# Weight loads of a fused attention and feed-forward kernel: from GpSimd DMAs that cast to SyncE DMAs with a cast on VectorE and ScalarE

## The chip, the cores and the metric

The kernel runs on one core of one Trainium2 chip. A core has five engines with queues of their own: TensorE (PE, matmuls; PEld is its weight load), VectorE (DVE), ScalarE (ACT), GpSimd (POOL) and SyncE (SP), and 16 DMA engines. Each engine takes its instructions in order and waits on semaphores. The metric is the time of one execution on the device in microseconds; the median of seven runs is given. Less is better.

## The reference

Block-wise decaying linear attention over 4 batches of 8 heads, 768 positions and 64 features, followed by a feed-forward layer with a Silu, 512 to 2048 to 512, over all 3072 tokens. Inputs and output are float32. `Dmask`, `lam_pow` and `rev_pow` hold powers of the head's decay `lam`: by distance within the block (zero ahead of the diagonal), by position from its start, and by position from its end; `lam_block` is the decay of a whole block.

```python
for b in range(nb):                       # blocks of 64 positions
    qb, kb, vb = (q[:, :, sl], k[:, :, sl], v[:, :, sl])
    intra = np.einsum('bhic,bhjc->bhij', qb, kb) * Dmask[None]
    intra = np.einsum('bhij,bhjd->bhid', intra, vb)
    inter = np.einsum('bhid,bhde->bhie', qb * lam_pow[None], kv_state)
    out[:, :, sl] = intra + inter
    kb_dec = kb * rev_pow[None]
    kv_state = lam_block[None, :, None, None] * kv_state + np.einsum('bhsd,bhse->bhde', kb_dec, vb)
...
x = out, heads side by side, one row a token
h = x @ w_in
g = h * (1.0 / (1.0 + np.exp(-h)))
return g @ w_out
```

## The kernel before

The 3072 tokens are 24 chunks of 128 (six to a batch) and ten groups of 256 or 384. For each chunk the kernel scales q and k by powers of the decay, transposes them, forms masked scores, adds the state's part and writes the attention output, in bf16 and transposed, into the group's tile `xt`. For each group it multiplies `xt` with `w_in_bf` (the up projection: L488 for groups of 256, L511 for groups of 384), applies Silu on ACT (L493, L515) into tiles `g`, and multiplies those with `w_out_bf` (the down projection, L537) into `o_ps`, which DVE copies to `ob` (L541) and SP stores.

The schedule is written out by hand. The opening, chunks 0 to 3 and the up projections of groups 0 and 1, is the string `ORDER`, in which each word is one operation: `qc:2,1,P` scales half 1 of the q pair of chunks 2 and 3 on POOL (L304), `kc` and `vc` do the same or a plain cast for k and v (L214, L152, L148; a last letter `s` means scaled, `u` unscaled), `tq` and `tk` transpose on PE (L369, L237), `qt` and `kt` copy the transposes out of PSUM, `s` forms scores (L251), `m` masks them on DVE (L257), `d` adds to the state (L289), `kv` copies it, `o` forms the output (L265, L270), `x` copies it to `xt`. `u:g,b,h` is 8 matmuls of 256 columns of the up projection for group g, block b of four output tiles, half h of the contraction; `g:` closes a bank with a Silu; `z:n` is n warm-up matmuls on zeros (L592). `w:i` loads piece i of w_in: 512 columns and half of the contraction, the piece that `u:g,b,h` with 2b + h = i needs. The letters D, A, P name the engine; the words give every engine's order, since each engine takes its own in the order of the string.

Weights are loaded by POOL with DMAs that cast from float32 to bf16 on the way, so they land where the matmuls read them (L144): eight w_in pieces of 512 KB in DRAM, four w_out pieces of 1 MB. q, k and v of chunks 0 to 5 come as pairs of blocks (`load_pair`, L187; 512 KB) or singly (`load_1`, L196; 256 KB) on SP, six pairs at the start. Two one-element DMAs from `xt` and `g` into a tile `gate` on SP (L620, L624) hold back the loads queued behind them until those tiles are written. The pair tiles are a ring of five and one tile with the tag `gate`.

After `ORDER` come the down projections of groups 0 and 1 (`down0(kk, ...)`: contraction tiles 4kk to 4kk+3) with the attention of chunks 4 and 5 between them: q and k scaled on POOL (L304, L309), `pe_tq`, `pe_tk` (L383), key copies into the zero-padded `ktbd` on DVE, scores `st_s` (L435), output `st_o` (L466). The padded tiles `ktbd` and `vpad` are zeroed first, two of each on DVE (L629, L630) and two on POOL (`clear_halves`, L164, L165); `clear_halves(0, 1)` comes again later for another layout. From chunk 6 on, `stretch` interleaves up projections, attention pieces and down projections by position; nothing of the change lies there.

```python
    for i in range(2):
        nc.vector.memset(ktbd[i], 0.0)
        nc.vector.memset(vpad[i], 0.0)
    clear_halves(2, 3)
...
    down0(0, 2, 3, 0, 1)
    prep_q1(4, 1), prep_q1(4, 0), prep_k(4), prep_k(5)
    down0(1, 2, 3, 0, 1)
    tq4 = pe_tq(4, "att")
```

Of the kernel before, what the change touches and what calls it, by code (L numbers as in the profile page):

```python
# [7 lines left out]
F32 = mybir.dt.float32  # L8
BF16 = mybir.dt.bfloat16
# [4 lines left out]

GROUPS = [256, 256, 256, 256, 256, 384, 384, 384, 384, 256]
# [4 lines left out]

ORDER = """
wl qc:0,0,P qc:0,1,D z:14 tq:0,att vc:0,0,P,s kc:0,0,D,u qt:0,0,D kc:0,1,A,u tk:0,1,h qt:0,1,A kt:0,1,D tk:0,0,att
qc:2,1,P kt:0,0,A z:2 s:0,1,att,o qc:2,0,P s:0,0,o,h vc:0,1,D,s d:0 m:0,1,0,D m:0,0,0,D m:0,1,1,D kv:0,A d:1 kc:2,1,D,u
kc:2,0,A,u m:0,0,1,D tq:2,att qt:2,1,D tk:2,0,o w:0 w:1 kv:1,A kt:2,0,D tk:2,1,h qt:2,0,A kt:2,1,A o:0,att,h vc:2,1,D,s
s:2,1,att,o m:2,1,1,D s:2,0,o,att m:2,0,1,D m:2,1,0,D vc:2,0,P,s x:0,A d:2 x:1,A u:0,0,0,h,h m:2,0,0,D w:2 kv:2,A d:3
kv:3,A u:0,0,1 g:0,0,1 o:2,att,att x:2,A w:3 w:4 x:3,D g:0,0,0 u:0,1,0,o,o u:0,1,1 g:0,1,0 g:0,1,1 u:1,0,0,h,h w:5
u:1,0,1 g:1,0,0 u:0,2,0,o,o u:0,2,1 w:6 g:1,0,1 g:0,2,1 w:7 u:1,3,0,h,h u:1,3,1 g:0,2,0 g:1,3,0 u:1,2,0,o,o u:1,2,1
g:1,3,1 g:1,2,0 g:1,2,1 u:0,3,0,h,h u:0,3,1 g:0,3,1 u:1,1,0,o,o u:1,1,1 g:1,1,1 g:1,1,0 g:0,3,0
# [4 lines left out]
def kernel(  # L33
# [10 lines left out]
    nc = tc.nc  # L44
# [29 lines left out]

    iota_i = const.tile([128, 2 * NB], mybir.dt.int32)
# [27 lines left out]
    NKV = 4  # L103
# [32 lines left out]

    def load_w(which, *pieces):
        for i in pieces:
            if which == "in":
                b, h = divmod(i, 2)  # L140
                dst, src = [t[:, 2 * h:2 * h + 2, 512 * b:512 * b + 512] for t in (w_in_bf, w_in_r)]
            else:
                dst, src = [t[:, 4 * i:4 * i + 4, :] for t in (w_out_bf, w_out_r)]
            nc.gpsimd.dma_start(out=dst, in_=src)  # L144
# [9 lines left out]
    mask2 = const.tile([128, BLK], F32)  # L154

# [24 lines left out]
    def load_q(c):  # L180

        load_pair(q, c, rawq, "gate")

    def load_pair(src, c, dst, tag="pair"):
        b, blk = divmod(c, NB)
        t = io.tile([128, H, 2, D], F32, name="pair", tag=tag, bufs={"pair": 5, "gate": 1}[tag])
        nc.sync.dma_start(out=t.rearrange("p h r d -> p h (r d)"),  # L187
                          in_=src[b, :, blk * BLK:(blk + 2) * BLK, :].rearrange("h (p r) d -> p h (r d)", r=2))
        dst[c] = t
# [9 lines left out]
    def load_k(c):  # L199
        rawk[c] = load_1(k, c, "kf", 6)  # L200

    def load_v(c):
        vraw[c] = load_1(v, c, "vf", 6)

    def load_c(c):
        rawq[c] = load_1(q, c, "qf", 4)
        load_k(c)
        load_v(c)
# [357 lines left out]
    for c in (0, 2):  # L566
        load_pair(q, c, rawq), load_pair(k, c, rawk), load_pair(v, c, vraw, "gate" if c else "pair")
# [20 lines left out]
    def op_z(n, tag="kv"):  # L588
# [8 lines left out]
        "w": lambda i: load_w("in", i), "u": op_u, "g": op_g, "z": op_z,  # L597
# [21 lines left out]
    gate = const.tile([128, 1], BF16)  # L619
    nc.sync.dma_start(out=gate[0:1, :], in_=xt[1][0:1, 0, 0:1])  # L620
    load_q(4)
    load_k(4), load_k(5)
    load_w("out", 0, 1, 2, 3)
    nc.sync.dma_start(out=gate[0:1, :], in_=gt[1, 0][0:1, 0:1])  # L624
    load_v(4), load_v(5)
    load_c(6)
    load_c(7)
    for i in range(2):
        nc.vector.memset(ktbd[i], 0.0)  # L629
        nc.vector.memset(vpad[i], 0.0)  # L630
    clear_halves(2, 3)
    for j in range(2):
        nc.gpsimd.tensor_copy(mask2[64 * j:64 * j + 64, :], mask[0:64, :])
# [15 lines left out]
    st_s(4)  # L649
    down0(2, 0, 1)  # L650
# [93 lines left out]
```

## Time and profile before

| | us |
|---|---|
| median of 7 runs | 219.43 |
| lowest, highest | 219.04, 222.48 |
| the profiled execution's own time | 222.45 |
| its span | 220.7 |
| PE busy in the span | 209.0 (95%) |
| DVE, ACT, POOL busy | 98.9, 95.7, 66.3 |
| first up-projection matmul starts | 17.64 |
| first down-projection matmul starts | 35.82 |

The span is from the first to the last recorded instruction; the rest of the execution's time lies around it. A line of the timeline gives the start in us, the duration in us, engine, source line, operation, output and inputs with their sizes, how many it stands for, and in brackets the idle time of the engine before it with what ended it. A window line gives a stretch, its length, the busy us of each engine with its number of instructions, the granted clock of TensorE, the mean busy share of the DMA engines (it can pass 1 where transfers overlap) and GB/s written. A DMA that casts counts with the bytes that it writes.

### The profile page before, as it was taken

The page shows a single profiled execution, that of the slowest core. Times are in us where ns is not written, and L with a number is a line of the kernel's source. Part 1 is how long each engine was busy: PE and PEld are TensorE (multiplying, and loading weights), DVE is VectorE, ACT ScalarE, POOL GpSimd, SP SyncE. Part 2 cuts the span into 40 slices and gives each one's busy share as a digit, 9 for nine tenths or more (in the row PEclk, how much of TensorE's full clock was granted, in tenths as well). Part 3 has the DMA queues.
Part 4 walks back from the last instruction along what each step waited for, and adds up shares of the span by engine and source line. Part 5 has one row for each costly group of instructions (what it writes and reads, how often), then busy time and mean ns, then how long its engine had stood idle before and what let it go on. Part 6 is the DMA issues. An engine that isn't in the chain of part 4 may idle for free.

```text
span 220.7 us, 4469 instructions
## 1 busy us (share of the span) xinstructions
PE 209.0 (95%) x1792; PEld 134.9 (61%) x1792; DVE 98.9 (45%) x239; ACT 95.7 (43%) x179; POOL 66.3 (30%) x83
## 2 busy tenths in 40 slices
PE   7878998999969999999999999999999999999994
PEld 2465775456846787776666566556655555566654
DVE  2693400067697467476665363624761333001121
ACT  4773554043542455554555454445444443432210
POOL 5599623144943333323403333202000000000000
PEclk9976999999997999999999999999999999999999
DMA  4979999987999999999988699928610110011112
GB/s 116 328 170 153 178 215 203 202 202 177 252 255 183 237 170 203 222 201 218 220 142 218 166 191 224 217 73 184 128 48 0 52 48 37 13 48 48 48 50 97
DMA packets 93209, 33.86 MB, mean 153 GB/s; under 512 B 78596, under 2 KB 90244, under 8 KB 93188
## 3 DMA queue, kind: packets, MB, share of 16 engines
q1 hardware_dynamic: 88756, 29.37, 57.6%
q0 software_dynamic: 4288, 4.20, 12.2%
q8 instruction: 14, 0.23, 0.5%
q14 instruction: 7, 0.06, 0.1%
q10 hardware_dynamic: 144, 0.00, 0.0%
HBM read 27.27 MB, written 6.29 MB: 152 GB/s over the span
## 4 chain that ended last, share of the span: by engine, by line
PE 76%; DMA 14%; DVE 4%; SPq 2%; POOL 1%; ACT 0%; issue 0%; DVEq 0%
PE o_ps L537 32%; PE h_ps L511 19%; PE h_ps L488 13%; DMA kf<-in_k_dram 9%; PE op L466 5%; PE sp L435 3%; DMA pair<-in_q_dram 3%; DMA w_in_bf<-in_moe_w_in_dram 2%; SPq L187 2%; DVE vpad L346 2%; PE kv_ps L411 2%; PE o_part L554 2%; POOL qb L304 1%; DVE ktbd L152 1%; POOL kb L309 0%
## 5 line engine op out<-in xcount | busy, mean ns | idle before, releaser
L537 PE MATMUL o_ps<-w_out_bf,g 128*128 128x512 bf16 x368 | 92.1, 380 | 0.8 <-ACT g L493 0.8
L537 PEld LDWEIGHTS <-g 128*128 128x128 bf16 x368 | 35.1, 98 | 32.0 <-issue 1.4
L515 ACT ACTIVATE g<-h_ps 128x384 bf16<-128x384 f32 x64 | 31.4, 490 | 46.7 <-PE h_ps L511 46.2
L488 PE MATMUL h_ps<-xt,w_in_bf 128*128 128x256 bf16 x384 | 49.7, 280 | 1.8 <-DMA w_in_bf<-in_moe_w_in_dram 1.8
L511 PE MATMUL h_ps<-xt,w_in_bf 128*128 128x384 bf16 x256 | 50.6, 326 | 0.0
L493 ACT ACTIVATE g<-h_ps 128x512 bf16<-128x512 f32 x48 | 27.9, 596 | 37.8 <-PE h_ps L488 37.7
L488 PEld LDWEIGHTS <-w_in_bf 128*128 128x128 bf16 x384 | 37.0, 100 | 10.1 <-DMA w_in_bf<-in_moe_w_in_dram 2.6
L315 POOL TENSOR_TENSOR qb<-qf,lam_fwd 128x512 bf16<-128x512 f32 x18 | 18.8, 1042 | 65.4 <-DMA qf<-in_q_dram 62.8
L541 DVE COPY ob<-o_ps 128x512 f32<-128x512 f32 x23 | 15.9, 691 | 47.7 <-PE o_ps L537 47.6
L511 PEld LDWEIGHTS <-w_in_bf 128*128 128x128 bf16 x256 | 23.7, 98 | 17.2
L442 DVE TENSOR_TENSOR ss<-sp,mask 128x512 bf16<-128x512 f32 (+1 forms) x40 | 21.0, 567 | 22.1 <-PE sp L435 22.0
L309 POOL TENSOR_TENSOR kb<-kf,lam_bwd 128x512 bf16<-128x512 f32 x20 | 20.9, 1045 | 7.9 <-DMA kf<-in_k_dram 7.8
L346 DVE COPY vpad<-vb 64x256 bf16<-64x256 bf16 x72 | 19.7, 273 | 1.6
L152 DVE CAST kvbd<-kv_ps 64x256 bf16<-64x256 f32 x32 | 13.5, 421 | 12.6 <-PE kv_ps L411 12.3
L474 ACT ACTIVATE xt<-op 128x512 bf16<-128x512 f32 x20 | 11.9, 597 | 13.7 <-PE op L466 13.0
L435 PEld LDWEIGHTS <-ktbd 128*128 128x128 bf16 x160 | 9.6, 100 | 5.0 <-DVE ktbd L152 1.9
L435 PE MATMUL sp<-qt,ktbd 128*128 128x128 bf16 (+1 forms) x160 | 10.6, 211 | 1.3 <-DVE ktbd L152 1.3
L466 PE MATMUL op<-ss,vpad 128*128 128x128 bf16 (+1 forms) x160 | 10.5, 208 | 1.2 <-DVE vpad L346 1.2
L148 ACT ACTIVATE vb<-vf 128x512 bf16<-128x512 f32 x18 | 11.2, 622 | 0.0
L152 DVE COPY ktbd<-tk 64x512 bf16<-64x512 bf16 x4 | 1.7, 422 | 20.6 <-PE tk L383 20.6
L466 PEld LDWEIGHTS <-vpad 128*128 128x128 bf16 x160 | 8.8, 98 | 1.9 <-DVE vpad L346 1.7
L152 DVE COPY ktbd<-kn 64x512 bf16<-64x512 bf16 x32 | 9.7, 302 | 0.4
(77 smaller groups left out, 124.2 us busy)
## 6 DMA issues: line engine op xcount, KB each, us to landing
out_dram<-ob SPq DMA_DIRECT2D x23, 256.0 KB, 3.2
kf<-in_k_dram SPq DMA_DIRECT2D x20, 256.0 KB, 4.0
vf<-in_v_dram SPq DMA_DIRECT2D x20, 256.0 KB, 4.4
qf<-in_q_dram SPq DMA_DIRECT2D x18, 256.0 KB, 3.4
w_in_bf<-in_moe_w_in_dram POOLq DMA_DIRECT2D x8, 256.0 KB, 8.3
w_out_bf<-in_moe_w_out_dram POOLq DMA_DIRECT2D x4, 512.0 KB, 18.5
pair<-in_q_dram SPq DMA_DIRECT2D x3, 512.0 KB, 6.1
pair<-in_k_dram SPq DMA_DIRECT2D x2, 512.0 KB, 6.3
```

Source lines behind the costliest of these rows:

```text
L152: nc.vector.tensor_copy(dst, src)
L309: VG[e].tensor_tensor(kb, rawk.pop(c).rearrange("s (p j) d -> s p j d", j=2), decay(lam_bwd, c % NB), op=AL.mult)
L315: nc.gpsimd.tensor_tensor(qb, rawq.pop(c).rearrange("s (p j) d -> s p j d", j=2), decay(lam_fwd, c % NB), op=AL.mult)
L346: nc.vector.tensor_copy(vh[64 * j:64 * j + 64, :, h, j, :], vb[64 * h:64 * h + 64, :, j, :])
L435: nc.tensor.matmul(sp[:, p, :], lhsT=lhsT, rhs=qt[:, p, a:], start=True, stop=True)
L442: VG[e].tensor_tensor(ss, sp, m[:, None, :n].to_broadcast([128, 4, n]), op=AL.mult)
L466: nc.tensor.matmul(dst, lhsT=lhsT, rhs=rhs, start=(i == 0), stop=(i >= len(terms) - NP), skip_group_check=True)
L488: nc.tensor.matmul(hps[g, i][:, a:a + 256], lhsT=w_in_bf[:, ko, m * 128:(m + 1) * 128], rhs=xt[g][:, ko, :], start=(ko == 0 and u == 0), s ...
L493: nc.scalar.activation(gg.rearrange("p u n -> p (u n)"), hps[g, i], AF.Silu)
L511: nc.tensor.matmul(hp[:, a:z], lhsT=w_in_bf[:, ko, m * 128:(m + 1) * 128], rhs=xt[g][:, ko, a:z], start=(ko == 0 and a == 0), stop=(ko == ...
L515: nc.scalar.activation(gg, hp[:, :n], AF.Silu)
L537: nc.tensor.matmul(o, lhsT=gt[g, ko][:, mt * BLK:(mt + 1) * BLK], rhs=w_out_bf[:, ko, :], start=(ko == 0), stop=(ko == KO_OUT - 1))
```

## The change

Weights come as float32 on SP's queue into the tiles of the pair ring and are cast to bf16 by DVE or ACT: `load_w` now only loads, `cast_w` casts. `LOADS` gives the order on SP: w_in pieces stand between and behind the q, k, v pairs, then six w_out pieces of 512 KB, then the loads of chunk 4 and so on. The ring has six tiles for all of these. In `ORDER` the word `w` is now a cast of half a piece with its engine, and the order of the opening is another one: key scaling comes first and chunk 0 scales k instead of v, there is one more pair of warm-up matmuls, and the up projections run in another sequence. The two gate DMAs are gone with their tile; a tile `pad` of 32 bytes a partition stands among the constants. The zero fills that POOL did before the down projection are done by DVE, and the copies of `mask` to `mask2` on POOL move to the front.

```diff
-wl qc:0,0,P qc:0,1,D z:14 tq:0,att vc:0,0,P,s kc:0,0,D,u qt:0,0,D kc:0,1,A,u tk:0,1,h qt:0,1,A kt:0,1,D tk:0,0,att
-qc:2,1,P kt:0,0,A z:2 s:0,1,att,o qc:2,0,P s:0,0,o,h vc:0,1,D,s d:0 m:0,1,0,D m:0,0,0,D m:0,1,1,D kv:0,A d:1 kc:2,1,D,u
-kc:2,0,A,u m:0,0,1,D tq:2,att qt:2,1,D tk:2,0,o w:0 w:1 kv:1,A kt:2,0,D tk:2,1,h qt:2,0,A kt:2,1,A o:0,att,h vc:2,1,D,s
-s:2,1,att,o m:2,1,1,D s:2,0,o,att m:2,0,1,D m:2,1,0,D vc:2,0,P,s x:0,A d:2 x:1,A u:0,0,0,h,h m:2,0,0,D w:2 kv:2,A d:3
-kv:3,A u:0,0,1 g:0,0,1 o:2,att,att x:2,A w:3 w:4 x:3,D g:0,0,0 u:0,1,0,o,o u:0,1,1 g:0,1,0 g:0,1,1 u:1,0,0,h,h w:5
-u:1,0,1 g:1,0,0 u:0,2,0,o,o u:0,2,1 w:6 g:1,0,1 g:0,2,1 w:7 u:1,3,0,h,h u:1,3,1 g:0,2,0 g:1,3,0 u:1,2,0,o,o u:1,2,1
-g:1,3,1 g:1,2,0 g:1,2,1 u:0,3,0,h,h u:0,3,1 g:0,3,1 u:1,1,0,o,o u:1,1,1 g:1,1,1 g:1,1,0 g:0,3,0
+wl kc:0,1,D,s z:14 tk:0,1,att qc:0,1,P vc:0,0,A,u qc:0,0,D z:2 tq:0,o kt:0,1,D qt:0,0,A qt:0,1,D kc:0,0,P,s tk:0,0,o z:2
+s:0,1,att,h qc:2,1,P m:0,1,0,D m:0,1,1,D vc:0,1,A,u kt:0,0,A d:0 kv:0,A s:0,0,o,o m:0,0,0,D kc:2,1,A,u d:1 m:0,0,1,D
+qc:2,0,P tq:2,h vc:2,0,P,s w:0,1,D kc:2,0,A,u tk:2,1,att kt:2,1,D qt:2,0,A o:0,h,att w:0,0,D qt:2,1,A vc:2,1,P,s tk:2,0,o
+x:0,A s:2,1,att,o x:1,D m:2,1,0,D kt:2,0,A u:0,0,0,h,h s:2,0,att,att w:1,1,A w:1,0,D m:2,1,1,D u:0,0,1 w:2,0,D kv:1,A d:2
+w:2,1,A u:0,1,0,o,o m:2,0,1,D m:2,0,0,D kv:2,A w:3,1,D d:3 kv:3,D g:0,0,1 w:3,0,A o:2,att,att w:4,0,D u:0,1,1 g:0,0,0
+w:4,1,A x:3,D x:2,A u:0,2,0,h,h w:5,0,D w:5,1,D g:0,1,1 u:0,2,1 g:0,1,0 w:7,0,D g:0,2,0 w:6,1,D g:0,2,1 u:1,1,0,o,o
+u:1,1,1 g:1,1,0 g:1,1,1 u:1,0,0,h,h w:6,0,D u:1,0,1 g:1,0,0 w:7,1,D g:1,0,1 u:0,3,0,o,o u:0,3,1 g:0,3,0 u:1,3,0,h,h
+u:1,3,1 g:0,3,1 g:1,3,1 g:1,3,0 u:1,2,0,o,o u:1,2,1 g:1,2,1 g:1,2,0
...
+LOADS = "Q0 K0 V0 Q2 K2 W0 V2 W1 W2 W3 W4 W5 W6 W7"
...
+    pad = const.tile([128, PAD], mybir.dt.uint8, name="pad")
...
+    wtmp = {}
+
+    def w_piece(which, i, a, b):
+        if which == "in":
+            c, h = divmod(i, 2)
+            return slice(2 * h + a, 2 * h + b), slice(512 * c, 512 * c + 512)
+        return slice(2 * i + a, 2 * i + b), slice(0, DM)
+
     def load_w(which, *pieces):
         for i in pieces:
-            if which == "in":
-                b, h = divmod(i, 2)
-                dst, src = [t[:, 2 * h:2 * h + 2, 512 * b:512 * b + 512] for t in (w_in_bf, w_in_r)]
-            else:
-                dst, src = [t[:, 4 * i:4 * i + 4, :] for t in (w_out_bf, w_out_r)]
-            nc.gpsimd.dma_start(out=dst, in_=src)
+            ko, f = w_piece(which, i, 0, 2)
+            t = io.tile([128, 2, 512], F32, name="pair", tag="pair", bufs=6)
+            nc.sync.dma_start(out=t, in_=(w_in_r if which == "in" else w_out_r)[:, ko, f])
+            wtmp[which, i] = t
+
+    def cast_w(which, i, e="D", part=None):
+        a, b = (0, 2) if part is None else (part, part + 1)
+        ko, f = w_piece(which, i, a, b)
+        move(e, (w_in_bf if which == "in" else w_out_bf)[:, ko, f], wtmp[which, i][:, a:b, :])
...
     mask2 = const.tile([128, BLK], F32)
+    for j in range(2):
+        nc.gpsimd.tensor_copy(mask2[64 * j:64 * j + 64, :], mask[0:64, :])
...
-        load_pair(q, c, rawq, "gate")
-
-    def load_pair(src, c, dst, tag="pair"):
+        load_pair(q, c, rawq)
+
+    def load_pair(src, c, dst):
         b, blk = divmod(c, NB)
-        t = io.tile([128, H, 2, D], F32, name="pair", tag=tag, bufs={"pair": 5, "gate": 1}[tag])
+        t = io.tile([128, H, 2, D], F32, name="pair", tag="pair", bufs=6)
...
-    for c in (0, 2):
-        load_pair(q, c, rawq), load_pair(k, c, rawk), load_pair(v, c, vraw, "gate" if c else "pair")
+    for word in LOADS.split():
+        if word[0] == "W":
+            load_w("in", int(word[1]))
+        else:
+            load_pair(*{"Q": (q, int(word[1]), rawq), "K": (k, int(word[1]), rawk), "V": (v, int(word[1]), vraw)}[word[0]])
+    load_w("out", *range(6))
+    load_q(4)
+    load_k(4), load_k(5)
+    load_w("out", 6, 7)
+    load_v(4), load_v(5)
+    load_c(6)
+    load_c(7)
...
-        "w": lambda i: load_w("in", i), "u": op_u, "g": op_g, "z": op_z,
+        "w": lambda i, h, e: cast_w("in", i, e, h), "u": op_u, "g": op_g, "z": op_z,
...
-    gate = const.tile([128, 1], BF16)
-    nc.sync.dma_start(out=gate[0:1, :], in_=xt[1][0:1, 0, 0:1])
-    load_q(4)
-    load_k(4), load_k(5)
-    load_w("out", 0, 1, 2, 3)
-    nc.sync.dma_start(out=gate[0:1, :], in_=gt[1, 0][0:1, 0:1])
-    load_v(4), load_v(5)
-    load_c(6)
-    load_c(7)
-    for i in range(2):
+    for i in range(6):
+        cast_w("out", i)
+    for i in range(NKV):
         nc.vector.memset(ktbd[i], 0.0)
         nc.vector.memset(vpad[i], 0.0)
-    clear_halves(2, 3)
-    for j in range(2):
-        nc.gpsimd.tensor_copy(mask2[64 * j:64 * j + 64, :], mask[0:64, :])
...
     st_s(4)
+    cast_w("out", 6), cast_w("out", 7, "A")
     down0(2, 0, 1)
```

## The prediction

> **What bounds the kernel now.** I read the page's parts 1 and 2 first, then the chain of waits, then the windows and the timeline of the first 70 us. Columns of part 2 are 40 slices of 5.5 us.
>
> ```profile
> span 220.7 us, 4469 instructions
> PE   7878998999969999999999999999999999999994
> DMA  4979999987999999999988699928610110011112
> PE 76%; DMA 14%; DVE 4%; SPq 2%; POOL 1%; ACT 0%; issue 0%; DVEq 0%
> ```
>
> From about 70 us TensorE is never idle by more than an issue gap, and the waits after 75 us name no wait of PE at all. So the end moves only by what PE loses or gains before 70 us: a microsecond won there is one won at the end. The change touches only that part. The windows of 2 us (columns: stretch, its length, busy us and instructions of PE, weight loads, DVE, ACT, POOL, then granted clock, DMA share, GB/s written) show the opening:
>
> ```profile
> 8.00:10.00 2.00, 1.87 (x34) 1.28 (x34) 1.57 (x4) 1.41 (x3) 0.77 (x1) 1.00 1.08 317
> ...
> 12.00:14.00 2.00, 1.59 (x36) 1.44 (x35) 2.00 (x6) 1.39 (x3) 2.00 (x3) 1.00 0.64 191
> 14.00:16.00 2.00, 1.97 (x67) 1.65 (x66) 2.00 (x4) 1.89 (x4) 1.98 (x3) 0.50 0.71 83
> 16.00:18.00 2.00, 1.03 (x30) 0.82 (x22) 2.00 (x4) 1.03 (x3) 2.00 (x4) 0.50 0.85 124
> ```
>
> The DMA engines, full until 12 us, fall to 0.64 to 0.85 until 18 us: the six q, k, v pairs have landed and the first weights, issued by POOL at 12.74 behind its own tensor work, have not. The first up-projection matmul waits for them, and later ones again, as the timeline says:
>
> ```profile
> 12.74 1.61 POOL L144 DMA_DIRECT2D w_in_bf<-in_moe_w_in_dram  x2
> ...
> 17.64 1.89 PE L488 MATMUL h_ps<-xt,w_in_bf 128*128 128x256 bf16 x8 [0.97 <-DMA w_in_bf<-in_moe_w_in_dram]
> ...
> 29.69 6.29 PE L488 MATMUL h_ps<-xt,w_in_bf 128*128 128x256 bf16 x56 [0.44 <-DMA w_in_bf<-in_moe_w_in_dram]
> ...
> 37.64 6.20 PE L537 MATMUL o_ps<-w_out_bf,g 128*128 128x512 bf16 x28 [0.80 <-ACT g L493]
> ...
> 46.44 0.40 PE L383 MATMUL tk<-ident,kb 128*128 128x128 bf16 x4 [0.20 <-POOL kb L309]
> ```
>
> The 128 matmuls of the opening's up projection ("u" items) run from 17.64 to 35.8, 18.2 us, though at the undisturbed pace of 0.87 us per 8 they are 14.0. DVE shows 0.00 busy from 30 to 44 us.
>
> **What the skill says.** "DMA: Bandwidth & Descriptors", section "Issuing engines are not separate DMA queues": all queues run on the same 16 engines, so a move from POOL to SP adds no bandwidth. The trace agrees: the share is 1.19 to 1.23 in nearly every window from 24 to 42 us with both queues in use. "SBUF — State Buffer", section "SBUF: two separate sides": VectorE in a two-port mode, or with two SBUF inputs, and GpSimd exclude each other for a whole instruction. The trace agrees: L214 on DVE took 1.55 and 1.72 us beside a POOL operation where the same form at L304 took 0.69. "TensorE: Matmul & The Clock Gate", Part 1: the array falls to half clock after an idle window of about 3.4 us. The trace shows 0.50 between 14 and 20 us, where 8 matmuls took 1.89 instead of 0.87.
>
> **The change part by part.** Sizes: 512 KB is one unit (a q, k or v pair, a w_in piece, a new w_out piece).
>
> 1. Loads on SP. Readers in the trace are released by K0 at 7.55, V0 at 9.23, Q2 at 10.75, K2 at 12.49, V2 by 14.3: 1.6 us a unit, the n-th landing near 4.4 + 1.6n. After the change nothing interrupts this stream: W0 is n=6 (14.0), V2 15.6, W1 17.2, then one each 1.6 us to W7 at 26.8, the first six w_out pieces 28.4 to 36.4, Q4 38.0, K4 and K5 39 and 40, the last w_out pieces 43.2. It can be quicker: from 24 to 44 us the trace wrote about 205 GB/s, near 4.1 MB; less Q4, K4 and K5 (1.05 MB) these are some 3.05 MB of cast weights, read as twice that, so about 7.15 MB read in 20 us, 355 GB/s and 1.5 us a unit. I work with 1.6 and keep 1.5 as the good end. The 8 + 4 POOL issues of 0.74 us vanish from POOL's queue; two stood before the k, v work of chunk 2. Both gate copies on SP go too.
>
> 2. Staging ring. Five pair tiles and one gate tile, filled seven times before, become six tiles filled 23 times; SP waits in order until the piece in a slot has been cast. By the readers' times: W2 waits for Q2's two POOL multiplies (10.75 + 2.08 = 12.9), W4 for V2's (15.6 + 2.08 = 17.7), W6 for W0's casts (about 16). Each is before the stream has used up the three units already queued (4.8 us), so I count nothing. A slot may be held 6 x 1.6 = 9.6 us.
>
> 3. Start of attention. On DVE the multiply of K0 now stands before that of Q0, so Q0's half waits until 7.55 instead of running at 6.27; with a POOL multiply of 1.04 in its way it ends near 10.0 (before: 7.0). Transposes 10.4, ACT and DVE copies 11.0, scores 11.2 (before 9.68): 1.5 us late. Four masks of 0.68 on DVE from 11.6 end at 14.3, output matmuls near 15.0, the x copies, behind two casts on DVE, at 16.6. W0 is cast by 15.9. So the first u begins at 16.6, against 17.64: 1.0 us gained. The added pair of warm matmuls (about 0.6) fills a PE wait.
>
> 4. Casts. 12 of w_in on DVE x 0.56 (row of the 128x512 cast, 0.535 to 0.591) = 6.8 us; 4 on ACT x 0.62 = 2.5; 7 of w_out on DVE, 128x1024, bounded by 0.59 and twice 0.56: I take 1.1, sum 7.9; one on ACT, 1.1. Not one is free by nature: they lie on the way from landing to matmul. But each costs PE only its lag where PE waits for that piece. Until about 25 us it does: u of piece W1 near 17.95, W2 19.4, o of chunk 2 20.8, W3 21.6, W4 22.6, W5 24.8. From there PE works through the u items of group 1, ending near 34.4 (ten items of 0.87 and 0.9 of waits for W6 and W7 after 24.8), or 33.8 with units of 1.5 us. Against 35.8 that is 1.4 to 2.0 gained.
>
> 5. Down projection. Before, its fifth matmul waits from 36.7 to 37.64 for the last Silu to free a bank; the new order closes those g items an earlier block ahead, so this 0.9 goes. Then 40 matmuls of 0.216 and 16 transposes (0.9) lead to the last key transpose: 34.4 + 9.5 = 43.9 against 46.44 + 0.2. W_out casts are ready in time (piece 5: 36.4 + 1.1 = 37.5, needed at 41.8).
>
> 6. Zero fills. Four POOL fills of 0.97 go from a time when POOL waits 7.9 us for Q4 afterwards: worth nothing. Four DVE fills of 0.49 are added, behind the casts: 8 fills end at 37.5 + 3.9 = 41.4. The copies of chunk 4's keys stand behind them, wanted at 42.9. Hidden with 1.5 us to spare. Q4 and both K cost POOL 2.08 + 2.08 after 38.0: 42.2, wanted at 43.7, also hidden.
>
> 7. The 256-byte boundaries. The removed gate tile occupied one 32-byte slot ahead of the weights; the added pad is 32 bytes. In the two built programs the weight, pair, k, v, q and output tiles have equal addresses, all multiples of 256 already. Only masks and padded k, v tiles move. This part does nothing to DMA: 0.
>
> Sum: 1.4 (u end) + 0.9 (bank wait) + 0.4 (the key transpose stood at 46.44, though the four matmuls begun at 45.22 end, at 0.216 each, at 46.1) = 2.7 at the slow unit; 3.3 at the fast one. I take 3.0. Later loads (chunks 6, 7) come earlier by as much, since the same stream brings them. PE's stalls between 57 and 66 us (waits on ktbd and vpad, 2.6 us) I leave as they are.
>
> The profiled execution has span 220.7 and own time 222.45, 1.75 around it; it would become 219.45. The median of the seven runs is 219.43; the profiled one also shows clock 0.66 between 65 and 70 us. I set the same difference against the median: 216.4.
>
> **Rivals.**
> (a) Ring and in-order casts starve the stream; slower. A slot is held from issue to landing (some 4.4 us without backlog, from the 4.0 and 4.4 of k and v issues) plus cast wait plus cast 1.1. To lose, K5 must be multiplied at 46.4 instead of 42.2, less the 1.5 spare that costs nothing at first: 4.2 us over 15 units, so 1.9 us each, a hold of 11.3 us, a cast wait of nearly 6 us. At a unit of 2.1 us K5 comes 7.5 late and the end 3.3 later than before: 222.7. For: cast of W6 stands behind the first half of W7 on DVE, and casts stand among attention steps. Against: step 4's waits are below 2 us.
> (b) The gain is mostly eaten: attention starts later still, because DVE and POOL collide on K0, and PE at half clock runs the W1 to W4 items at 1.75 us each. Then u ends near 35.5, 0.3 is won there and 0.9 at the bank wait: 218.2.
> (c) Two stalls more go: with chunks 6 and 7 landed early, POOL's multiplies no longer collide with DVE's vpad copies (L346, four in 3.92 us near 59): 2 us more, 214.4.
> (d) Everything cancels within 0.2%: 219.4.
>
> **How the numbers follow.** Forecast 0.55, (a) 0.17, (b) 0.13, (c) 0.10, (d) 0.05. The likeliest case's own range is 215.1 to 217.7. Leaving out the upper part of (a) and the lower of (c), the range is 214.4 to 219.9. What can be told from no change is 0.2%, 0.44 us. Faster 0.55 + 0.13 + 0.10 = 0.78, same 0.05, slower 0.17.
>
> **What would show it.** Right: DMA share stays at 1 from 4 to 45 us; first u near 16.6; down projection from 33 to 34.5 with no wait after its fourth matmul; last key transpose near 43. Wrong: SP waiting on casts for microseconds, a drop of the DMA share between 14 and 40 us, PE waiting on ktbd behind the fills, or a first u after 18.

## The result and the profile after

| | before | after |
|---|---|---|
| median, us | 220.1 (217.89 to 223.05, 60 runs) | 217.74 (216.63 to 219.96, 23 runs) |
| ratio | | 0.9907, 95% interval 0.9891 to 0.9923 |
| the profiled execution's own time, us | 222.45 | 217.2 |
| its span, us | 220.7 | 215.5 |

The ratio and its interval leave out executions more than 1.5% above the fastest of their kernel, so the ratio is not quite the quotient of the medians. The change makes the kernel 0.93% faster, about 2.05 us. The two profiled executions are 5.2 us apart, two and a half times as much. So one of the two is not a usual one, and before any line of them is compared this has to be settled: the first experiment does it.

The page of the changed kernel (its first line, the DMA row of the 40 slices, which are 5.4 us each here, and the engines' shares of the chain that ended last):

```profile
span 215.5 us, 4511 instructions
...
DMA  4999999998997779998999999839311011011112
...
PE 84%; DVE 6%; DMA 6%; ACT 2%; issue 1%; SPq 0%; DVEq 0%
```

The 7 in the third slice of the DMA row of before (11 to 16.5 us) is a 9 now, and the DMA's share of the chain falls from 14% to 6%: the end is seldom traced back to a load now. The windows of the opening (stretch, its length, busy us and instructions of PE, weight loads, DVE, ACT, POOL, then granted clock, DMA share, GB/s written) say the same:

```profile
12.00:14.00 2.00, 1.47 (x51) 1.24 (x51) 1.19 (x2) 1.29 (x5) 0.70 (x1) 0.70 1.04 338
14.00:16.00 2.00, 2.00 (x66) 1.77 (x66) 2.00 (x6) 1.97 (x4) 0.51 (x1) 1.00 1.13 383
16.00:18.00 2.00, 1.21 (x25) 0.90 (x26) 2.00 (x4) 1.99 (x6) 1.72 (x2) 1.00 1.01 384
```

The share is 1.01 to 1.13 where it was 0.64 to 0.85, and the clock is full from 14 us on, where in the first profile it was a half until 20. Only from 18 to 20 us does the share drop, to 0.77. The timeline of the changed kernel, DVE and PE lines in order of time:

```profile
7.62 0.69 DVE L233 TENSOR_TENSOR kp<-pair,lam_bwd 128x512 bf16<-128x512 f32 x1 [2.70 <-DMA pair<-in_k_dram]
8.22 1.53 DVE L323 TENSOR_TENSOR qb<-pair,lam_fwd 128x512 bf16<-128x512 f32 x1
12.81 2.48 DVE L276 TENSOR_TENSOR ss<-sp,mask_p 128x512 bf16<-128x512 f32 x4 [0.88 <-PE sp L270]
15.88 0.94 DVE L169 CAST w_in_bf<-pair 128x512 bf16<-128x512 f32 x1
16.74 0.68 DVE L169 CAST xt<-op 128x512 bf16<-128x512 f32 x1
17.47 1.05 PE L507 MATMUL h_ps<-xt,w_in_bf 128*128 128x256 bf16 x8 [0.79 <-DVE xt L169]
22.62 12.02 PE L507 MATMUL h_ps<-xt,w_in_bf 128*128 128x256 bf16 x104
34.48 7.07 PE L556 MATMUL o_ps<-w_out_bf,g 128*128 128x512 bf16 x32
43.78 0.39 PE L402 MATMUL tk<-ident,kb 128*128 128x128 bf16 x4
```

Of the four PE waits that the prediction showed, the last three are gone. The first up-projection item starts hardly earlier than before (17.47 against 17.64) and now waits for the copy of the attention output to `xt`, not for weights. The remaining 104 matmuls from 22.62 on are one line. That hides waits too short for a line of their own: near 24.6 and 25.0 us two matmuls start 0.37 and 0.34 us behind the one before, where 0.11 is usual, because the casts of W5 are late. The waits of the weight loads show them (waiting engine and line, whom it waited for, us in total, times, longest):

```profile
PEld L507 <- DVE w_in_bf L169: 0.6, 2, 0.4
```

So about 0.5 us is still lost to weights there, and none behind it. The down projection's first 32 matmuls are one line too, so the wait for a Silu's bank is gone. The last key transpose of the opening, that of chunk 5, stands at 43.78.

### The profile page after: what moved, and what is told of

It is laid out like the page before. It is cut to its first block, busy times and chain, and to the rows that moved or that the text cites. A ratio compares the mean times of both kernels' runs of the same rounds, so it can differ in the third digit from the quotient of the medians.

```text
span 215.5 us, 4511 instructions
## 1 busy us (share of the span) xinstructions
PE 206.3 (96%) x1794; PEld 133.3 (62%) x1794; DVE 115.2 (53%) x261; ACT 98.6 (46%) x184; POOL 55.2 (26%) x68
## 4 chain that ended last, share of the span: by engine, by line
PE 84%; DVE 6%; DMA 6%; ACT 2%; issue 1%; SPq 0%; DVEq 0%
PE o_ps L556 36%; PE h_ps L530 19%; PE h_ps L507 15%; PE op L485 5%; PE sp L454 3%; DMA pair<-in_k_dram 3%; DMA pair<-in_moe_w_in_dram 3%; PE o_part L573 2%; PE kv_ps L430 2%; DVE ktbd L169 1%; DVE ss L461 1%; PE tq L388 1%; DVE qb L323 1%; DVE vpad L365 1%; ACT kvbd L165 1%
## 5 line engine op out<-in xcount | busy, mean ns | idle before, releaser
L556 PEld LDWEIGHTS <-g 128*128 128x128 bf16 x368 | 35.0, 98 | 31.2 <-issue 0.4
L507 PE MATMUL h_ps<-xt,w_in_bf 128*128 128x256 bf16 x384 | 47.9, 273 | 0.9 <-DVE xt L169 0.8
L507 PEld LDWEIGHTS <-w_in_bf 128*128 128x128 bf16 x384 | 36.1, 98 | 8.4 <-DVE xt L169 0.9
L530 PEld LDWEIGHTS <-w_in_bf 128*128 128x128 bf16 x256 | 23.7, 98 | 17.2
L461 DVE TENSOR_TENSOR ss<-sp,mask 128x512 bf16<-128x512 f32 (+1 forms) x40 | 21.0, 566 | 16.6 <-PE sp L454 16.3
L365 DVE COPY vpad<-vb 64x256 bf16<-64x256 bf16 x72 | 20.4, 283 | 1.6
L169 DVE CAST kvbd<-kv_ps 64x256 bf16<-64x256 f32 x34 | 14.3, 421 | 11.9 <-PE kv_ps L430 10.7
L169 DVE COPY ktbd<-kn 64x512 bf16<-64x512 bf16 x32 | 15.6, 486 | 0.4
L323 POOL TENSOR_TENSOR qb<-pair,lam_fwd 128x512 bf16<-128x512 f32 x5 | 5.1, 1041 | 21.9 <-DMA pair<-in_q_dram 20.3
```

The lines of the kernel that those rows point to most:

```text
L169: nc.vector.tensor_copy(dst, src)
L365: nc.vector.tensor_copy(vh[64 * j:64 * j + 64, :, h, j, :], vb[64 * h:64 * h + 64, :, j, :])
L461: VG[e].tensor_tensor(ss, sp, m[:, None, :n].to_broadcast([128, 4, n]), op=AL.mult)
L507: nc.tensor.matmul(hps[g, i][:, a:a + 256], lhsT=w_in_bf[:, ko, m * 128:(m + 1) * 128], rhs=xt[g][:, ko, :], start=(ko == 0 and u == 0), s ...
L530: nc.tensor.matmul(hp[:, a:z], lhsT=w_in_bf[:, ko, m * 128:(m + 1) * 128], rhs=xt[g][:, ko, a:z], start=(ko == 0 and a == 0), stop=(ko == ...
L556: nc.tensor.matmul(o, lhsT=gt[g, ko][:, mt * BLK:(mt + 1) * BLK], rhs=w_out_bf[:, ko, :], start=(ko == 0), stop=(ko == KO_OUT - 1))
```

## The experiments

Four marks on PE tell the runs apart: the start of the first up-projection item, the start of the down projection, the key transpose of chunk 5 (the second `tk` on `kb`), and what is left of the span behind it. All kernels compute the whole output.

| run | first item | down projection | key transpose | span | behind it | ratio to before, 95% interval |
|---|---|---|---|---|---|---|
| before, first profile | 17.64 | 35.82 | 46.44 | 220.7 | 174.3 | |
| before_again | 17.86 | 35.31 | 45.57 | 217.3 | 171.7 | |
| after | 17.47 | 34.48 | 43.78 | 215.5 | 171.7 | 0.9907, 0.9891 to 0.9923 |
| order_alone | 17.57 | 35.72 | 45.48 | 218.1 | 172.6 | 1.0010, 0.9986 to 1.0034 |
| loads_alone | 18.58 | 37.28 | 47.54 | 219.9 | 172.4 | 1.0060, 1.0038 to 1.0082 |
| loads_early | 18.82 | 36.40 | 46.66 | 218.6 | 171.9 | 1.0002, 0.9979 to 1.0025 |
| fills_pool | 17.30 | 34.84 | 44.14 | 215.4 | 171.3 | 0.9890, 0.9841 to 0.9939 |
| no_pad | 18.52 | 35.70 | 45.00 | 217.4 | 172.4 | 1.0001, 0.9979 to 1.0023 |
| before_off | 18.29 | 36.81 | 47.07 | 218.1 | 171.0 | 1.0059, 1.0039 to 1.0079 |
| pad_64 | 17.65 | 38.37 | 47.67 | 220.1 | 172.4 | 1.0002, 0.9983 to 1.0022 |
| pad_128 | 17.47 | 34.65 | 43.95 | 218.2 | 174.2 | 0.9997, 0.9974 to 1.0020 |
| q_first | 15.54 | 33.37 | 42.67 | 215.4 | 172.7 | 0.9874, 0.9839 to 0.9909 |
| best2 | 16.14 | 33.76 | 43.06 | 214.6 | 171.5 | 0.9891, 0.9854 to 0.9929 |
| best3 | 16.99 | 37.17 | 46.47 | 217.7 | 171.2 | 0.9886, 0.9847 to 0.9925 |

A mark comes from one execution each; the ratio comes from many. Where they disagree, as in before_off, whose profiled execution (219.83) is over 1 us below that kernel's median of 221.0, the ratio decides. The profiled executions of pad_64 and best3 lie 2.1 and 1.4 us above their medians. The ratios of fills_pool, q_first, best2 and best3 rest on three to four executions, so their intervals are wide.

**The kernel before once more.** No edit.

> The kernel before once more, for a second profile. The first two profiles differ by 5.2 us of span, the medians by some 2.2. If the change is worth what the medians say, the last key transpose of chunk 5 stands again near 46.4 us (43.8 in the changed kernel) and the stretch from there to the end is about 171.7, as in the changed kernel, instead of 174.3. If the later part too is really shortened by the change, this stretch stays near 174.

Measured: 218.96 us of its own, span 217.3. The timeline of this second execution of the kernel before:

```profile
17.86 1.89 PE L488 MATMUL h_ps<-xt,w_in_bf 128*128 128x256 bf16 x8 [1.55 <-DMA w_in_bf<-in_moe_w_in_dram]
...
20.25 1.43 PE L488 MATMUL h_ps<-xt,w_in_bf 128*128 128x256 bf16 x8
...
29.19 6.29 PE L488 MATMUL h_ps<-xt,w_in_bf 128*128 128x256 bf16 x56 [0.27 <-DMA w_in_bf<-in_moe_w_in_dram]
37.14 6.20 PE L537 MATMUL o_ps<-w_out_bf,g 128*128 128x512 bf16 x28 [0.80 <-ACT g L493]
45.57 0.39 PE L383 MATMUL tk<-ident,kb 128*128 128x128 bf16 x4
```

The waits for weights and the 0.80 for the Silu's bank are there as in the first profile. The wait for chunk 5's keys at the last line is not, and behind it 171.7 us remain, as many as after the change. So of the 5.2 us between the first two profiles, 3.4 belonged to that one execution of the kernel before. Against an ordinary one, the changed kernel gains 45.57 - 43.78 = 1.8 us by the key transpose, 0.83 in the up projection and 0.96 in the down projection, and nothing behind it. This is the 2 us of the medians within what two single executions can show.

The 0.83 of the up projection is all won before 22.6 us. At 22.62 the changed kernel has 104 matmuls left and takes 11.86 us for them; at 22.63 before_again has 112 left and takes 12.68, which is the same pace of 0.91 us for 8. Ahead of that, the first item of before_again begins 0.39 later, and its first two items take 1.89 and 1.43 us, where those of the changed kernel take 1.05 each. These are the windows of before_again with its granted clock (third number from the end); the changed kernel has 1.00 in both:

```profile
15.00:20.00 5.00, 3.21 (x68) 2.23 (x70) 3.34 (x5) 1.82 (x5) 5.00 (x8) 0.77 1.16 167
20.00:25.00 5.00, 5.00 (x82) 4.20 (x79) 2.06 (x4) 3.29 (x7) 3.79 (x6) 0.89 1.12 154
```

The lowered clock thus costs these two items 1.2 us, more than the 0.83; the changed kernel gives some of it back at W5's casts and in attention matmuls that its order puts between the items. From 15 to 20 us all five profiles with the old order show a clock of 0.50 to 0.84, and of the nine with the new order all but no_pad (0.71) show 1.00. No run changes the clock alone, so how much of the gain is the clock's and how much the weights' is not measured.

**The new order with the old loads.** The weights stay on POOL's queue with the cast in the DMA; `ORDER` is the new one, its casts taken out and the issues put where POOL has room:

```diff
-kc:2,0,A,u m:0,0,1,D tq:2,att qt:2,1,D tk:2,0,o w:0 w:1 kv:1,A kt:2,0,D tk:2,1,h qt:2,0,A kt:2,1,A o:0,att,h vc:2,1,D,s
+qc:2,0,P tq:2,h w:0 w:1 vc:2,0,P,s kc:2,0,A,u tk:2,1,att kt:2,1,D qt:2,0,A o:0,h,att qt:2,1,A vc:2,1,P,s w:2 w:3 w:4 w:5 w:6 w:7 tk:2,0,o
```

> The new order of the opening, with the weights still loaded by GpSimd DMAs that cast, with the gates and the fills of before. If the uninterrupted stream on SyncE makes the gain, the first weights still come near 17.6, the DMA share still dips at 12 to 18 us, and only the bank wait before the down projection goes: ratio to the kernel before 0.995 to 0.999. If the order makes the gain, ratio 0.991 as for the whole change.

Measured: 1.0010, no difference. The wait for the bank is gone, as predicted. But the down projection starts 0.41 later than in before_again: the clock is 1.00 from 15 to 25 us, yet three items wait 0.79, 0.20 and 0.24 us for weights. And another wait stands behind that of the bank. The timeline of this kernel between 43 and 46 us:

```profile
43.28 2.04 POOL L310 TENSOR_TENSOR kb<-kf,lam_bwd 128x512 bf16<-128x512 f32 x2 [3.59 <-DMA kf<-in_k_dram]
...
44.38 0.40 PE L384 MATMUL tk<-ident,kb 128*128 128x128 bf16 x4 [0.29 <-POOL kb L310]
```

POOL waited 3.59 us for the keys of chunk 4 to land, and PE for POOL. The loads of chunk 4 stand in the same stream behind the weights, and that stream is as late as before: its DMA share between 10 and 15 us is 0.73 in this run, 1.09 after the change. The first key transpose stands 8.7 us behind the start of the down projection, in the changed kernel 8.2. So the 0.96 of the bank wait is used up by 0.41 in the up projection and some 0.45 at the keys.

**The new loads with the old order.** The old `ORDER`, float32 loads on SP; each piece's two casts stand shortly ahead of its first item. The line with the third and later pieces:

```diff
-kv:3,A u:0,0,1 g:0,0,1 o:2,att,att x:2,A w:3 w:4 x:3,D g:0,0,0 u:0,1,0,o,o u:0,1,1 g:0,1,0 g:0,1,1 u:1,0,0,h,h w:5
+kv:3,A u:0,0,1 g:0,0,1 o:2,att,att x:2,A w:2,0,D w:2,1,A x:3,D g:0,0,0 u:0,1,0,o,o w:3,0,D w:3,1,A u:0,1,1 g:0,1,0 g:0,1,1 u:1,0,0,h,h w:4,0,D w:4,1,D
```

> The order of before, with the weights as float32 on SyncE, the pair ring and the casts put just ahead of the matmuls that need them. If the stream makes the gain: first up projection near 16, down projection near 34.5 with the bank wait of 0.9 still there, ratio 0.992 to 0.997. If the order makes it: ratio 0.999 or above, because casts on DVE and ACT then stand in the way.

Measured: 1.0060, slower. The longest waits of SP's queue before 45 us in this kernel (waiting engine and line, whom it waited for, us in total, times, longest), and then PE's waits in its timeline:

```profile
SPq L154 <- ACT w_in_bf L164: 4.7, 1, 4.7
SPq L154 <- DVE w_in_bf L168: 4.2, 5, 1.6
```

```profile
18.58 1.27 PE L506 MATMUL h_ps<-xt,w_in_bf 128*128 128x256 bf16 x8 [1.30 <-DVE w_in_bf L168]
25.02 12.43 PE L506 MATMUL h_ps<-xt,w_in_bf 128*128 128x256 bf16 x111 [1.00 <-ACT w_in_bf L164]
39.10 6.20 PE L555 MATMUL o_ps<-w_out_bf,g 128*128 128x512 bf16 x28 [0.80 <-ACT g L511]
...
52.48 1.02 PE L555 MATMUL o_ps<-w_out_bf,g 128*128 128x512 bf16 x4 [1.94 <-DVE w_out_bf L168]
```

This is the mechanism of the prediction's rival (a). W2's second cast stands behind the output copy of chunk 2 on ACT, so its ring slot is held and SP, which takes its queue in order, waits 4.7 us; the DMA share falls to 0.81 between 25 and 30 us, and the items and the last output weights wait in turn. The old wait for the bank is still there, and the first two items take 1.27 and 1.89 us at a lowered clock (0.83 from 15 to 20 us, 0.66 from 20 to 25).

**The same with the casts earlier.** To separate the placement of the casts from the old order itself, W2's casts were moved ahead of chunk 2's output and the others an item forward. The same line:

```diff
-kv:3,A u:0,0,1 g:0,0,1 o:2,att,att x:2,A w:2,0,D w:2,1,A x:3,D g:0,0,0 u:0,1,0,o,o w:3,0,D w:3,1,A u:0,1,1 g:0,1,0 g:0,1,1 u:1,0,0,h,h w:4,0,D w:4,1,D
+kv:3,A u:0,0,1 g:0,0,1 w:2,0,D w:2,1,A o:2,att,att w:3,0,D x:2,A x:3,D w:3,1,D g:0,0,0 u:0,1,0,o,o w:4,0,D w:4,1,A u:0,1,1 g:0,1,0 g:0,1,1 w:5,0,D w:5,1,D u:1,0,0,h,h
```

> The loads alone once more: the order of work of the kernel before, the weights as float32 on SyncE's queue, but each piece's two casts placed one up-projection item or more ahead of their first use, so that no cast stands behind a wait of the output matmuls. Theory (the loads alone failed through the ring, because casts placed late held slots): SP's longest wait on a cast falls below 3 us, the DMA share stays above 0.9 until 40 us, up projection ends at 34.5 to 35.3, the 0.8 wait for the last Silu's bank stays, ratio 0.993 to 0.998. Rival (the order of before cannot feed the casts wherever they stand): the first up-projection item after 18, its end after 36.5, ratio 1.000 or more.

Measured: 1.0002. SP's longest wait on a cast of ACT falls from 4.7 to 3.2 us and the time by 0.6%, so placement was what made the loads alone slower than the kernel before. Nothing is gained over the kernel before, though. PE in this kernel:

```profile
18.82 1.55 PE L506 MATMUL h_ps<-xt,w_in_bf 128*128 128x256 bf16 x8 [1.65 <-DVE w_in_bf L168]
...
38.23 6.20 PE L555 MATMUL o_ps<-w_out_bf,g 128*128 128x512 bf16 x28 [0.80 <-ACT g L511]
```

W0's cast stands behind three masks on DVE that the old order puts there, and the first item waits for it. In the new order the cast is ahead of these masks. The first two items again run at a lowered clock (0.84 and 0.69 in the two windows) and take 1.55 and 1.89 us. So the rival's number came true, for its reason in part: one placement was tried, and another within the old order may do better.

**The zero fills back on POOL.**

```diff
-    for i in range(NKV):
+    for i in range(2):
         nc.vector.memset(ktbd[i], 0.0)
         nc.vector.memset(vpad[i], 0.0)
+    clear_halves(2, 3)
```

> The changed kernel with the zero fills of the third and fourth key and value buffers back on GpSimd. Theory (the move is worth nothing): ratio 0.989 to 0.993, POOL's fills lie before Q4's landing at 36.6, and the keys of chunks 4 and 5 are multiplied on POOL no later than before, chunk-5 key transpose 43.8. Rival (the fills cost something on POOL): its multiplies of Q4 and the keys begin later, PE waits for kb, and the transpose comes 0.5 us or more later, ratio 0.994 or more.

Measured: 0.9890 (0.9841 to 0.9939), as the changed kernel. The four fills lie on POOL between 17.5 and 21.7 us, and POOL then waits 15.2 us for Q4. The move is worth nothing that this run could show; its interval would hide half a per cent.

**The pad left out.**

```diff
-    pad = const.tile([128, PAD], mybir.dt.uint8, name="pad")
```

> The changed kernel without its 32-byte pad tile, so that every tile a DMA writes begins 32 bytes below a 256-byte boundary. In the kernel before, the gate tile's slot did what the pad does now, so the change itself moved nothing here; the run asks what the boundary is worth. Theory (worth nothing): a ratio to the kernel before of 0.989 to 0.993, as the changed kernel, weights landing 1.3 to 1.5 us apart, last key transpose of chunk 5 near 43.8. Rival (the boundary matters to the DMA engines): landings further apart, 1.6 us or more, the DMA share at 1 for longer, the key transpose after 44.5, ratio 0.994 or more.

Measured: 1.0001. The rival is right: without these 32 bytes the whole gain is gone. The first issues of SP's queue in the changed kernel (start, duration; the first two issues, ahead of these, take 0.45 and 0.56 us, and the later ones longer, as if they waited for earlier pieces to move), then the same without the pad:

```profile
4.56 1.52 SPq L206 DMA_DIRECT2D pair<-in_q_dram  x1
6.12 1.45 SPq L206 DMA_DIRECT2D pair<-in_k_dram  x1
```

```profile
4.73 1.60 SPq L205 DMA_DIRECT2D pair<-in_q_dram  x1
6.37 1.74 SPq L205 DMA_DIRECT2D pair<-in_k_dram  x1
```

The issue of K2 goes from 1.45 to 1.74 us, a fifth more. By their first readers K0 and Q2, two pieces apart, land at 7.62 and 10.66 with the pad and at 8.34 and 11.90 without: 1.52 and 1.78 us a piece. The pages' queue lines (packets, MB, share of 16 engines) of the two, with the pad and without, show the same bytes in more DMA time:

```profile
q1 hardware_dynamic: 93104, 37.76, 70.8%
```

```profile
q1 hardware_dynamic: 93104, 37.76, 77.7%
```

The first item starts 1.05 later, the down projection and the key transpose 1.22 later, and 0.7 is lost behind that, 1.9 in the span.

**Which boundary.** The pad at 96 and at 160 bytes puts the tiles 64 and 128 bytes above a 256-byte boundary; a 32-byte tile added to the kernel before puts its tiles 32 above one:

```diff
-PAD = 32
+PAD = 96
```

> The changed kernel with a pad of 96 bytes, so that all tiles that DMAs write begin 64 bytes above a 256-byte boundary (without the pad they began at 224, which cost the whole gain). Theory (a tile must lie on a 64-byte boundary, and any will do): as the changed kernel, ratio 0.988 to 0.993, the loads' queue (q1) at 66 to 71% of the 16 engines' span, key transpose of chunk 5 near 43.8. Rival (only a coarser boundary will do): q1 at 75% or more, key transpose near 45, ratio 0.997 or more.

> The same with a pad of 160 bytes, so that these tiles begin 128 bytes above a 256-byte boundary. If 64 bytes are enough, this is as the changed kernel too (0.988 to 0.993, q1 66 to 71%). If the run at 64 is slow and this one is fast, the boundary is one of 128 bytes; if both are slow (0.997 or more, q1 at 75% or more) it is one of 256.

> The kernel before with a 32-byte tile added ahead of the others, so that its DMA tiles begin 32 bytes above a 256-byte boundary in place of on one. Theory (the boundary matters to every load, and the kernel before had it by the gate's slot): its queues take longer too, q1 63% or more in place of 57.6%, and as its up projection waits for weights, ratio 1.004 to 1.012. Rival (it matters only where the stream of loads is what PE waits for, which the order of before is less than that of the change): q1 longer, but ratio 0.998 to 1.003.

Measured: 1.0002 (0.9983 to 1.0022) at 64, 0.9997 (0.9974 to 1.0020) at 128, and 1.0059 for the kernel before moved off its boundary. Neither a 64-byte nor a 128-byte boundary will do, and 256 is enough: in the built programs on the boundary these tiles begin at odd multiples of 256. The issue of K2 takes 1.74 at 64, 1.74 at 128, 1.73 at 32 and 1.74 without the pad (224), against 1.45 in all runs on the boundary. Queue q1 takes 76.2% and 73.5% in the first two, and 68.3% for 57.6% in the kernel before. (In the execution profiled at 128 the opening is hardly late, 43.95 at the key transpose, and the time is lost behind it, at waits on `ktbd` and `vpad` of 2.7 us; where the slower stream shows is not the same in every execution. The 76.2% is from the longest execution of pad_64.) In before_off the theory held and its rival fell: the boundary was worth 0.6% to the kernel before as well, which had it through the slot that the gate tile took. (The added tile also moves the masks and the padded tiles, which no DMA writes, from 224 bytes above a boundary onto one.)

**Q0 ahead of K0.** The prediction's step 3 saw Q0's half wait on DVE behind K0's. Q0's half on DVE is scaled first here, its transposes lead, and the two pairs of warm-up matmuls stand together; in the next line, not shown, chunk 0's value copy `vc:0,0,A,u` moves behind `kt:0,0,A`:

```diff
-wl kc:0,1,D,s z:14 tk:0,1,att qc:0,1,P vc:0,0,A,u qc:0,0,D z:2 tq:0,o kt:0,1,D qt:0,0,A qt:0,1,D kc:0,0,P,s tk:0,0,o z:2
+wl qc:0,0,D kc:0,1,D,s z:14 qc:0,1,P tq:0,o qt:0,0,A qt:0,1,D tk:0,1,att kt:0,1,D kc:0,0,P,s tk:0,0,o z:4
```

> The changed kernel, but Q0 is scaled on DVE before K0, and transposed first. If the late start of attention (first up-projection matmul at 17.47 instead of the predicted 16.6) costs time at the end, the scores of chunk 0 come near 9.5 instead of 12.06, the first up projection at 15 to 16 and the ratio falls to 0.986 to 0.989. If the weights' arrival paces TensorE until 25 us anyway, the start moves but the ratio stays at 0.990 to 0.992.

Measured: 0.9874, not told apart from the change's 0.9907 by the intervals. PE in this kernel:

```profile
15.54 1.05 PE L507 MATMUL h_ps<-xt,w_in_bf 128*128 128x256 bf16 x8
...
46.11 1.02 PE L556 MATMUL o_ps<-w_out_bf,g 128*128 128x512 bf16 x4 [0.43 <-DVE w_out_bf L169]
...
58.98 0.55 PE L485 MATMUL op<-ss,vpad 128*128 128x128 bf16 x8 [0.41 <-DVE vpad L365]
61.33 0.51 PE L454 MATMUL sp<-qt,ktbd 128*128 128x128 bf16 x8 [0.93 <-DVE ktbd L169]
```

The first item comes 1.9 us earlier and waits less than 0.15 us for `xt`, the key transpose comes 1.1 earlier, and 1.0 of that is lost again behind it. The three waits shown are 0.43, 0.41 and 0.93, where the changed kernel has 0.27, none and 0.16: at the cast of the seventh output piece, and at DVE copies, some of which take longer here (four `vpad` copies in 2.97 us, 1.59 after the change).

**Those waits removed.** To this kernel two more edits were added, the seventh piece's cast ahead of the key copies on DVE, and the clears between groups on DVE in place of POOL:

```diff
+    cast_w("out", 6)
...
-    cast_w("out", 6), cast_w("out", 7, "A")
+    cast_w("out", 7, "A")
...
-            nc.gpsimd.memset(ktbd[i], 0.0)
-            nc.gpsimd.memset(vpad[i], 0.0)
+            nc.vector.memset(ktbd[i], 0.0)
+            nc.vector.memset(vpad[i], 0.0)
```

> The changed kernel with three edits: both halves of Q0 multiplied before K0 (as in the run q_first), the cast of the seventh output weight piece ahead of the key copies on VectorE, and the clears between groups on VectorE in place of GpSimd. Theory: the 0.3 to 0.4 wait for that cast near 46 us goes, POOL's work for chunks 8 and 9 no longer falls on VectorE's padded value copies near 59, which then take about 1 us for four and not 3; ratio 0.981 to 0.985. Rival (the clears on VectorE come in front of these copies and cost what they save): ratio 0.986 to 0.990, with waits on vpad or ktbd of as much as before between 45 and 66 us.

Measured: 0.9891, the rival's number. In its profile the wait for the cast of the seventh output piece is gone, the `vpad` copies take 1.74 and the span is the shortest of all, 214.6. Over its four runs it is not shown to be faster than the change.

**W1 loaded ahead of V2.** Two words of `LOADS` change places on top of that:

```diff
-LOADS = "Q0 K0 V0 Q2 K2 W0 V2 W1 W2 W3 W4 W5 W6 W7"
+LOADS = "Q0 K0 V0 Q2 K2 W0 W1 V2 W2 W3 W4 W5 W6 W7"
```

> The changed kernel with the three edits of the run best2 (both halves of Q0 ahead of K0, the seventh output weight piece's cast ahead of the key copies, the clears between groups on VectorE) and a fourth: the piece W1 is loaded ahead of V2. Theory: the second up-projection item no longer waits 0.8 us for W1 behind V2, its items end near 33.0 in place of 33.8, and the end comes as much earlier, ratio 0.982 to 0.987. Rival (V2 is then late: the output matmuls of chunk 2 wait for its values): items end at 33.8 or later, ratio 0.987 to 0.992.

Measured: 0.9886 (0.9847 to 0.9925), between both. Its six runs go from 215.69 to 219.53, and the one profiled took 219.38, so it shows the bad end. The timeline of that execution, POOL, SP and DVE:

```profile
18.08 2.04 POOL L233 TENSOR_TENSOR vp<-pair,lam_bwd 128x512 bf16<-128x512 f32 x2 [5.28 <-DMA pair<-in_v_dram]
...
20.15 1.97 SPq L155 DMA_DIRECT2D pair<-in_moe_w_in_dram  x4
...
25.60 0.43 DVE L169 CAST w_in_bf<-pair 128x512 bf16<-128x512 f32 x1 [2.75 <-DMA pair<-in_moe_w_in_dram]
```

V2 lands one piece later, its multiplies on POOL end at 18.08 + 2.04 = 20.12, only then is its slot free, and SP's next issue is at 20.15; DVE waits 2.75 us for a weight piece, and PE waits 2.1 us at 26.09. In the changed kernel the same multiplies end at 17.72 and SP issues at 17.74. So in this execution the ring cost PE two microseconds. That it does so usually is not shown: the ratio is that of the change.

No version was shown to be faster than the change itself.

## Why the prediction was right, point by point

- **Direction and mechanism**: right. The weights' stream no longer waits for POOL to issue it, and the gain is won in the up projection and at the bank wait, as the steps had it. Some of the numbers came out by errors that cancel, as steps 1, 2 and 4 show.
- **Step 1, loads**: the unit of 1.6 us held up to W7, which was there at 27.16 (predicted 26.8). The output pieces came faster, their casts released at 29.64, 30.90, 32.22 and 33.50, 1.29 apart, and so Q4 was there at 36.56 (38.0).
- **Step 2, ring**: its dates were right and its cost was not nothing. V2's multiplies on POOL end at 17.72 (predicted 17.7) and SP's next issue follows at 17.74. By then the stream had run low: the DMA share is 0.77 from 18 to 20 us, with 196 GB/s after 384 in the window before, and SP's longest waits are 2.5 us for casts on DVE and 2.3 for POOL. Both, such a drop and such waits, the prediction had named as signs of being wrong. Faster pieces behind it (380 to 401 GB/s from 24 to 28 us) made up for most of the loss. It cost PE little, the 0.5 us at W5 at most. The margin is thin: loads_alone lost by it, and one execution of best3. The rival (a) was a real mechanism in the wrong place.
- **Step 3, start of attention**: half right. Q0's half on DVE did wait behind K0 and took 1.53 beside POOL, ending at 9.75 (predicted 10.0). The rest was too quick: the masks ended at 15.3 instead of 14.3, a weight cast ahead of the `xt` copy took 0.94 beside POOL, and the first item came at 17.47, not 16.6. Of the 1.0 us gained there, 0.2 were seen against the first profile, 0.4 against before_again.
- **Step 4, casts**: the end of the items at 34.48 was forecast at 34.4, and that is luck. The later start was made up by W5's item, 24.64 for 24.8, since PE waited less on the way. Behind it the prediction counts ten items, but with W5's own there are eleven, 0.87 more; and it counts 0.9 of waits for W6 and W7 that did not come. Counted with eleven items its end would have been 35.3, and its sum at the slow unit 1.8 instead of 2.7. Casts were cheaper than priced, mostly 0.42 for 0.56 and 0.69 for 1.1 us.
- **Step 5, down projection**: right. The bank wait went, and the key transpose stands at 43.78 for 43.9.
- **Step 6, fills**: right within the interval of fills_pool.
- **Step 7, boundaries**: right as a comparison of these two kernels, and its "does nothing to DMA" is no more than that. The pad keeps what the removed gate tile had given; without it the forecast gain is lost whole.
- **The sum**: 3.0 us forecast, 2.05 measured. The term mis-sized is the baseline from which the gains were taken. The 0.4 of the key wait, and 0.5 of the 35.82 at which the items ended, belonged to one execution; before_again has no such key wait and ends its items at 35.31. The same forecast of 43.9 set against 45.57 gives 1.7.
- **The clock**: the sum has no term for it. The prediction took the half clock of the first profile as a fact of the kernel before and gave it a part only in rival (b), but the first two items of before_again lose 1.2 us by it. The idle window of about 3.4 us that the prediction quotes for it is not seen as a wait of PE: in before_again PE waits 2.17 us up to 7.96 and the clock stays full, and it waits 1.55 up to 17.86 and the clock falls, to 0.91 from 16 to 18 us and 0.50 from 18 to 20. What lowers it here stays open.
- **The rivals**: (b) was right that attention would start late. It was wrong that PE would do W1 to W4 at half clock, 1.75 us an item: they took 1.05 or less. Its 1.2 us of gain and the forecast's 3.0 lie about equally far from the measured 2.05. (c) fell: of the 2.6 us of waits between 57 and 66 us of the first profile before_again has 1.3 and the changed kernel 0.6, and these two have the same time left behind the key transpose.

The order and the loads need each other: with the order alone PE waits for weights and then for keys, and with the loads alone the casts come late and the clock is low. And both need the tiles on their boundary. What was not tried is a new order found for the old loads, or another placement of casts within the old order.

## What to carry to other kernels

Before a sum is made against one profiled execution, compare its own time with the median of the runs; when it is 3 us over, as here, take a second profile, or the waits that only that one shows are counted as gains. Compare the granted clock of each stage too, since a wait and a lowered clock both make an item late. A timeline line without a wait can hide short ones: compare its duration with its count. Where a staging ring feeds an in-order queue, look for the reader that frees a slot last, not for the average, and put its cast ahead of whatever waits on its engine. When a small tile is removed or added, look at the addresses of all tiles behind it: here 32 bytes decided over the whole gain.

## What the runs showed of the hardware

For pieces of 512 KB in rows of 512 bytes, the issue of K2, the fifth in the queue, took 1.45 us when the tiles in SBUF began on a 256-byte boundary and 1.73 to 1.74 when they began 32, 64, 128 or 224 bytes above one. By their first readers the pieces landed 1.52 us apart in the changed kernel and 1.78 without the pad. The output weights, 512 KB in rows of 2 KB, were (33.50 - 29.64) / 3 = 1.29 us apart on the boundary and (37.01 - 31.56) / 4 = 1.36 off it, by the releases of their casts in one execution each.

The traces also hold every single packet. Between 4 and 12 us, 99% of the 512-byte packets of the changed kernel took 27 ns. Off the boundary only 27 to 37% did, and most others took up to 40; the mean of those under 60 ns is 31.1 at 32 bytes, 31.1 at 64, 31.2 at 128 and 32.3 at 224, against 27.0. Of the 2-KB packets before 45 us, 94% took 84 ns on the boundary and 54% without the pad, with means of 84.3 and 87.1 for those under 120 ns. So a row off the boundary does not pay a fixed amount: some show no loss, and the 2-KB rows pay less on average than the 512-byte rows.

The Trainium skill has the rule on its page "DMA: Bandwidth & Descriptors", section "How a descriptor splits into AXI transactions": a descriptor is cut into pieces of 256 bytes, and one that doesn't start on a multiple of 256 fetches from the boundary below, which costs beats for the unused bytes. That there is a cost, and that 256 is the boundary, agrees with these runs; the prediction had not drawn on it. In size they differ. Worked out by the page's count, an estimate, a 512-byte row of 16 beats needs 18 at offset 64 and 23 at 224, while the measured means of 31.1 and 32.3 ns are almost the same. The page speaks of reads, and here the tiles are written. Why some rows pay and others don't is not shown.
